# Reading order of the first matmul operand in a run: blocks from the end, in a chunked and in a Strassen-type product

## The chip, the cores and the metric

The kernel runs on one core of one Trainium2 chip. The metric is the device time of one execution in microseconds. The kernel before took 860.09 us (median of 3 runs, 858.67 to 861.0).

## The reference

```python
kv  = einsum('bhsd,bhse->bhde', k, v)             # (8, 8, 64, 64)
out = einsum('bhsd,bhde->bhse', q, kv)            # (8, 8, 576, 64)
rms = sqrt(mean(out * out, axis=-1) + 1e-6)
x   = (out / rms * g_norm)  ->  (4608, 512)       # heads side by side
h   = x @ w_in                                    # (4608, 2048)
g   = maximum(h, 0) + log1p(exp(-abs(h)))         # softplus
y   = g @ w_out                                   # (4608, 512)
```

Everything is 32 bits wide. The two large products need more precision than one pass gives, so every operand of them is kept as three parts (a high part, a rest and a combination of both), and every product is three matmuls that add up in PSUM.

## The kernel before

**Attention.** For each batch, `k` and `v` are multiplied into `kv` (line 696). For each tile of 128 tokens `q` is multiplied by `kv` (line 720), each head's row is normalised (VectorE, ScalarE, GpSimd), and the rows are turned so that features lie on the partitions (line 738 or VectorE). The turned x goes to DRAM and comes back split into three parts.

**The feed-forward block** has 2048 hidden columns in 16 chunks of 128, and is done in three passes over the tokens.

- The first phase (`step`) goes through 12 blocks of 384 tokens. Four blocks take 4 chunks each and eight take 6, so there are 64 steps, in the text "chunks". A chunk's first product `mm1` (line 864) is 12 matmuls of 128x384: 3 parts (`i`) times 4 slices of the 512 features (`kd`), numbered m = 0 to 11, all into one bank. ScalarE and VectorE make softplus and its three parts. The second product `mm2` (line 871) is 9 matmuls of 128x512, 3 for each of 3 tiles of tokens, and adds up over the chunks in banks of its own. In the steady part TensorE runs `mm1` of one chunk, `mm2` of an earlier one, `mm1` of the next, and so on.
- The two Strassen phases (`wide_step`) take the other chunks, two at a time, on 512 tokens. The first product is done with seven products of half size in place of eight (`product`, line 1066): each is 6 matmuls of 128x256, three parts (`m`) times two slices (`kd`). Between them ScalarE and VectorE copy and add banks. The second product (`mm2` inside `wide_step`, line 1137) is 3 matmuls of 128x512 for each of 2 chunks and 4 tiles of tokens. Products and second products are interleaved: a run of one, two or more products (6, 12 and more matmuls of 256 columns) stands between runs of second products. The text calls such a run of products a visit.

**The order of the work** is written by a planner (`Plan.order`): each task has an engine, an estimated duration, a position and the buffers it takes and gives, and the planner simulates the engines and issues the tasks in the order of its simulated starts. The instructions of each engine are then issued in that order. Within a task such as `mm1`, `product` or `mm2` the matmuls follow each other as the loops say.

**Reading orders.** Both the moving operand and the bank that is written can be run through in blocks from the end. The helper is

```python
def from_the_end(x, w):
    return x.rearrange("p (b w) -> p b w", w=w)[:, ::-1] if w else x
```

With `w` = 0 the columns are taken forward. With `w` = 16 they are taken in blocks of 16 words, last block first, each block forward. The same order is used for the operand and for the bank, so each result lands in the column where it belongs. Before the change, `mm1` reads m = 0 to 10 forward and m = 11 with `w` = 1 (word by word backward); the first-phase `mm2` reads forward; a Strassen product alternates `w` = 16 and 8 with `kd`; the Strassen `mm2` uses `w` = 128. Each matmul has its own weight load, which runs beside the matmul before it.

Further lines that the prediction names: 952 (`prime`, one 512-column matmul with the identity that clears a bank), 776, 525 and 526 (small matmuls of the attention part and of the weight preparation).

Of the kernel before, what the change touches and what calls it, by code (L numbers as in the profile page):

```python
# [18 lines left out]
P = 128  # L19
# [22 lines left out]
def from_the_end(x, w):  # L42

    return x.rearrange("p (b w) -> p b w", w=w)[:, ::-1] if w else x
# [16 lines left out]
class Plan:  # L61
# [19 lines left out]
    def slot(self, ring):  # L81
        return Slot(ring)

    def add(self, engine, ns, run, after=(), pos=0.0, take=(), give=(), size=0, behind=None, follows=None, kind="all"):
        pos, behind = round(pos, 4), None if behind is None else round(behind, 4)
        t = Task(engine, ns, run, [a for a in after if a is not None], pos, list(take), list(give), size)
        for s in t.give:
            s.readers += 1
        self.tasks.append(t)
        t.follows = follows  # L90
        t.behind = behind
        t.kind = kind
        return t
# [113 lines left out]
def kernel(  # L207
# [24 lines left out]
    nc = tc.nc  # L232
# [5 lines left out]
    KD, KF = d_model // P, d_ff // P  # L238
# [610 lines left out]
    def step(s):  # L849
        n, c = ORDER[s]  # L850
        cs = CHUNKS[n]
        h, g, gv = slot("h"), slot("g"), slot("gv")
        if c == cs[0]:
            sums[:] = [slot(f"s{i}") for i in range(TB)]
        xv, w_in, w_out = xv_slots[n], w_slots[0, c], w_slots[1, c]
        mine = list(sums)
        kept = c >= 4

        def mm1():
            hp = new(h, [P, NT])  # L860
            for m in range(3 * KD):
                i, kd = divmod(m, KD)
                w = 1 if m == 3 * KD - 1 else 0
                nc.tensor.matmul(from_the_end(hp, w), lhsT=w_in.tile[:, i, kd * P:(kd + 1) * P], rhs=from_the_end(xv.tile[:, i, kd], w),  # L864
                                 start=(m == 0), stop=(m == 3 * KD - 1))

        def mm2(i):
            if c == cs[0]:
                new(mine[i], [P, d_model])
            for m in range(3):  # L870
                nc.tensor.matmul(mine[i].tile, lhsT=gv.tile[:, m, i * P:(i + 1) * P], rhs=w_out.tile[:, m],  # L871
                                 start=(c == cs[0] and m == 0), stop=(c == cs[-1] and m == 2))

        def low():
            nc.vector.tensor_tensor(out=gv.tile[:, 1], in0=g.tile, in1=gv.tile.bitcast(F32)[:, 0], op=ALU.subtract)

        def less():
            f32 = gv.tile.bitcast(F32)
            nc.vector.scalar_tensor_tensor(out=gv.tile[:, 2], in0=f32[:, 1], scalar=-RADIX, in1=f32[:, 0],
                                           op0=ALU.mult, op1=ALU.add)  # L880

        a = add("PE", 2100, mm1, x_split[n] + factors_done[0, c] + [m for _, m in mm1s[-1:]] +
                (factors_done[1, ORDER[s - 2][1]] if s > 1 else []), s, [h],
                ([xv] if c == cs[-1] else []) + ([w_in] if s == last_step[c] and c != 4 else []))
        mm1s.append((s, a))
        a = add("ACT", 490, lambda: nc.scalar.activation(new(g, [P, NT]), h.tile, func=AF.Softplus, scale=1.0 + E),  # L886
                [a], s, [g], [h])
        a = add("ACT", 530, lambda: nc.scalar.activation(new(gv, [P, 3, NT], F32R)[:, 0], g.tile, func=AF.Copy, scale=DOWN),
                [a], s, [gv])
        a = add("DVE", 570, low, [a], s, [], [g])  # L890
        a = add("DVE", 570, less, [a], s)
        for i in range(TB):
            a2 = add("PE", 700, lambda i=i: mm2(i), [a] + factors_done[1, c] + [mm2s.get(i)], s + 1.5,
                     [mine[i]] if c == cs[0] else [],
                     [gv] + ([w_out] if s == last_step[c] and not kept else []))
            mm2s[i] = a2
            if c == cs[-1]:
                leave(0, n * TB + i, mine[i], a2, s + 1.5)
# [60 lines left out]
    def units_of(ph, n):  # L959
# [3 lines left out]
        for j, us in enumerate(GROUPS):  # L963
# [74 lines left out]
            for v, u in enumerate(us):  # L1038
                unit_slots[ph, n, u] = dst, v
                unit_done[ph, n, u] = [c]  # L1040

    PRODUCTS = [(0, 0), (1, 0), (0, 1), (1, 1), (2, 1), (2, 0), (3, 0)]

    def wide_step(k):
# [9 lines left out]
        def place(q):  # L1054
            return ab.tile[:, q // 2, q % 2 * HW:(q % 2 + 1) * HW]
# [3 lines left out]
        def product(u, q):  # L1059
            f, i = PRODUCTS[u]  # L1060
            w = forms[p][f].tile
            dst, v = unit_slots[ph, n, u]
            for m in range(3):
                for kd in range(2):
                    at = i * 2 * P + kd * P
                    nc.tensor.matmul(from_the_end(place(q), (16, 8)[kd]), lhsT=w[:, m, at:at + P],  # L1066
                                     rhs=from_the_end(dst.tile[:, m, v, kd] if u < 6 else dst.tile[:, m, kd], (16, 8)[kd]),
                                     start=(u == 0 and not m and not kd), stop=(m == 2 and kd == 1), skip_group_check=True)

        def multiply(u, q, after, pos, take=(), follows=None):  # L1070
            f = PRODUCTS[u][0]
            give = [unit_slots[ph, n, u][0]] if last else []
            if final and u in (2, 3, 5, 6):
                give.append(forms[p][f])
            return add("PE", 710, lambda: product(u, q), unit_done[ph, n, u] + forms_done[p][f] + list(after), pos, take, give,
                       follows=follows)
# [3 lines left out]
        def gt(dtype=F32):  # L1080
            if dtype not in held:
                held[dtype] = sb.tile([P, 2, WIDE], dtype, tag=f"g{gv.place}", name=f"g{gv.place}_{dtype == F32}")
            return held[dtype]

        def gvt(m, dtype=F32):
            y = gv.tile[:, m]
            return y if dtype == F32R else y.bitcast(F32)
# [8 lines left out]
        def begin():  # L1096
            new(ab, None)
            product(0, X)
# [31 lines left out]
            nc.vector.scalar_tensor_tensor(out=gt(F32R), in0=gvt(1), scalar=-RADIX, in1=gvt(0), op0=ALU.mult, op1=ALU.add)  # L1130

        def mm2(c, i):
            fresh = first and not c and ph < LAST
            if fresh:
                new(mine[i], [P, d_model])
            for m in range(3):
                nc.tensor.matmul(from_the_end(mine[i].tile, P), lhsT=(gvt(m, F32R) if m < 2 else gt(F32R))[:, c, i * P:(i + 1) * P],  # L1137
                                 rhs=from_the_end(outs[c].tile[:, m], P),
                                 start=fresh and not m, stop=(last and c == 1 and m == 2), skip_group_check=True)
# [21 lines left out]
        for c in range(2):  # L1161
            for i in range(TW):
                slot_pos = b + PACE + MM2[TW * c + i]
                a2 = add("PE", 700, lambda c=c, i=i: mm2(c, i),
                         [split_done[c]] + factors_done[1, 2 * p + c] + ([seeds[i]] if i in seeds and not c else []) +
                         ([before[i]] if c or not first else []), slot_pos, [mine[i]] if first and not c and ph < LAST else [], [gv] + ([outs[c]] if final else []))
                before[i] = a2
                if last and c:
                    leave(ph, TW * n + i, mine[i], a2, slot_pos)
# [98 lines left out]
```

## Time and profile before

| what | value |
|---|---|
| median of 3 runs | 860.09 us |
| lowest, highest run | 858.67, 861.0 us |
| profiled execution, time | 858.61 us |
| profiled execution, span from first to last instruction | 856.8 us |
| granted TensorE clock, mean | 1.000 |
| matmuls at line 864 (384 columns) | 768 |
| matmuls at line 871 (512 columns) | 576 |
| matmuls at line 1066 (256 columns) | 2016 |
| matmuls at line 1137 (512 columns) | 1152 |

All durations come from the profiled execution. The page lists the busy time of each engine, the chain of work that ended last (followed back from the last instruction), and groups of instructions by line with their tiles, shapes and counts. A line of the timeline has the start in microseconds from the span's start, the time that the group of successive instructions took to its last end, the engine, the line, the tiles and the count. Matmuls overlap: one starts before the one before it has ended, so the distance between two starts is what a matmul costs in a dense stream. The trace has each start to the nanosecond, and distances of single matmuls are from there. A few matmul records can be missing from a trace.

### The profile page before, as it was taken

What the parts mean: (1) busy time and instruction counts of PE and PEld (TensorE: products, weight loads), DVE (VectorE), ACT (ScalarE), POOL (GpSimd) and SP (SyncE); (2) the same over time, 40 slices, a digit from 0 to 9 for tenths busy, and PEclk for the clock granted to TensorE, in tenths of its full rate; (3) what the DMA queues carried; (4) which work ended last, traced back from release to release, by engine and by line L of the source; (5) the groups of instructions that cost most, each with busy time, mean ns of one, the idle gap of its engine ahead of it and who ended that gap; (6) DMA issues with size and microseconds to landing.
All of it is one profiled execution on the core that took longest, in us unless ns stands there. A gap on an engine that the chain in (4) does not pass through costs nothing.

```text
span 856.8 us, 17075 instructions
## 1 busy us (share of the span) xinstructions
PE 843.8 (98%) x6464; PEld 754.7 (88%) x6464; DVE 704.1 (82%) x995; ACT 520.2 (61%) x980; POOL 76.1 (9%) x79
## 2 busy tenths in 40 slices
PE   7899999999999999999999999999999999999998
PEld 5678898999898999998999999998999899999996
DVE  7988898888788889798898788878788766788873
ACT  6866665446344567776667665655868555566654
POOL 0342224111113300000000000000000000000000
PEclk9999999999999999999999999999999999999999
DMA  9998997778784755436645456645354753777864
GB/s 275 301 228 218 264 270 244 178 243 221 215 186 118 194 159 183 143 112 202 211 156 167 160 160 203 197 158 182 124 195 138 234 167 103 241 242 239 250 189 130
DMA packets 239778, 167.07 MB, mean 195 GB/s; under 512 B 106320, under 2 KB 198736, under 8 KB 239696
## 3 DMA queue, kind: packets, MB, share of 16 engines
q1 hardware_dynamic: 239392, 165.86, 65.8%
q8 instruction: 50, 0.82, 0.4%
q14 instruction: 32, 0.26, 0.1%
q10 hardware_dynamic: 304, 0.13, 0.1%
HBM read 112.98 MB, written 52.95 MB: 194 GB/s over the span
## 4 chain that ended last, share of the span: by engine, by line
PE 94%; DVE 2%; ACT 1%; DMA 1%; issue 1%; POOL 1%; SPq 0%; DVEq 0%; ACTq 0%
PE banks L1137 31%; PE banks L1066 28%; PE banks L871 16%; PE banks L864 15%; PE banks L720 2%; PE banks L696 2%; DMA loads<-in_v_dram 1%; DMA raw<-in_moe_w_in_dram 0%; PE banks L738 0%; POOL roots L728 0%; PE banks L1232 0%; DVE half L732 0%; DVE m L464 0%; DVE m L460 0%; DVE units L643 0%
## 5 line engine op out<-in xcount | busy, mean ns | idle before, releaser
L1137 PE MATMUL banks<-pieces,gv 128*128 128x512 f32 x768 | 236.8, 390 | 0.0
L1137 PE MATMUL banks<-pieces,g_False 128*128 128x512 f32 x384 | 149.4, 389 | 0.0
L1137 PEld LDWEIGHTS banks<-pieces,gv 128*128 128x128 f32 x768 | 132.5, 188 | 17.2 <-DVE banks L910 0.2
L864 PE MATMUL banks<-units,pieces 128*128 128x384 f32 x768 | 145.6, 338 | 0.0
L871 PE MATMUL banks<-pieces,gv 128*128 128x512 f32 x576 | 143.3, 393 | 0.0
L864 PEld LDWEIGHTS banks<-units,pieces 128*128 128x128 f32 x768 | 135.5, 188 | 4.5
L871 PEld LDWEIGHTS banks<-pieces,gv 128*128 128x128 f32 x576 | 106.2, 188 | 19.0
L1066 PEld LDWEIGHTS banks<-units,pieces 128*128 128x128 f32 x840 | 111.0, 188 | 6.5 <-ACT banks L1112 0.4
L1066 PE MATMUL banks<-units,pieces 128*128 128x256 f32 x840 | 115.2, 280 | 0.0
L886 ACT ACTIVATE half<-banks 128x384 f32<-128x384 f32 x64 | 31.4, 491 | 95.7 <-PE banks L864 89.8
L1127 DVE TENSOR_TENSOR gv<-g_True,gv 128x1024 fp32r<-128x1024 f32 x47 | 57.5, 1223 | 36.3 <-ACT gv L1124 36.3
L1137 PEld LDWEIGHTS banks<-pieces,g_False 128*128 128x128 f32 x384 | 72.1, 188 | 15.0
L1066 PEld LDWEIGHTS banks<-units,w 128*128 128x128 f32 x504 | 66.7, 188 | 3.7 <-ACT banks L1112 0.2
L1066 PE MATMUL banks<-units,w 128*128 128x256 f32 x504 | 69.6, 280 | 0.0
L728 POOL TENSOR_TENSOR roots<-roots,half 128x8 f32<-128x8 f32 x36 | 61.9, 1720 | 3.0
L1130 DVE SCALAR_TENSOR_TENSOR g_False<-gv 128x1024 fp32r<-128x1024 f32 x47 | 57.6, 1225 | 1.5
L1029 DVE TENSOR_TENSOR units<-loads,units 128x1024 fp32r<-128x1024 f32 x42 | 51.2, 1219 | 6.0 <-ACT units L1026 5.9
L1094 ACT ACTIVATE g_True<-banks 128x256 f32<-128x256 f32 x96 | 36.7, 384 | 30.6 <-PE banks L1066 29.9
L1116 DVE TENSOR_TENSOR g_True<-banks,g_True 128x512 f32<-128x512 f32 x48 | 33.1, 690 | 25.8 <-PE banks L1066 19.8
L931 ACT ACTIVATE m<-banks 128x512 f32<-128x512 f32 x72 | 42.1, 595 | 17.7 <-PE banks L1137 12.5
L1032 DVE SCALAR_TENSOR_TENSOR units<-units 128x1024 fp32r<-128x1024 f32 x42 | 51.4, 1224 | 1.7
L1026 ACT ACTIVATE units<-loads 128x1024 fp32r<-128x1024 f32 x42 | 44.4, 1056 | 12.7 <-PE banks L1066 10.1
(115 smaller groups left out, 1248.5 us busy)
## 6 DMA issues: line engine op xcount, KB each, us to landing
loads<-x SPq DMA_DIRECT2D x180, 128.0 KB, 2.7
part<-m SPq DMA_DIRECT2D x72, 256.0 KB, 2.9
m<-part SPq DMA_DIRECT2D x72, 256.0 KB, 3.5
loads<-form SPq DMA_DIRECT2D x45, 256.0 KB, 3.2
form<-loads SPq DMA_DIRECT2D x36, 256.0 KB, 3.0
raw<-in_moe_w_in_dram SPq DMA_DIRECT2D x16, 512.0 KB, 4.6
loads<-in_k_dram SPq DMA_DIRECT2D x32, 256.0 KB, 4.5
loads<-in_v_dram SPq DMA_DIRECT2D x32, 256.0 KB, 4.6
```

The lines of the kernel that those rows point to most:

```text
L728: nc.gpsimd.tensor_tensor(out=r.tile, in0=r.tile, in1=half, op=ALU.pow)
L864: nc.tensor.matmul(from_the_end(hp, w), lhsT=w_in.tile[:, i, kd * P:(kd + 1) * P], rhs=from_the_end(xv.tile[:, i, kd], w), start=(m == 0), ...
L871: nc.tensor.matmul(mine[i].tile, lhsT=gv.tile[:, m, i * P:(i + 1) * P], rhs=w_out.tile[:, m], start=(c == cs[0] and m == 0), stop=(c == cs ...
L931: a = add("ACT", 690 if ph == LAST else 600, lambda: nc.scalar.activation(new(ot, [P, d_model]), bank.tile, func=AF.Copy, scale=scale if p ...
L1026: nc.scalar.activation(part_of(0, F32R), xl.tile if m > 1 else xl.tile[:, 0], func=AF.Copy, scale=DOWN)
L1029: nc.vector.tensor_tensor(out=part_of(1, F32R), in0=xl.tile if m > 1 else xl.tile[:, 0], in1=part_of(0), op=ALU.subtract)
L1032: nc.vector.scalar_tensor_tensor(out=part_of(2, F32R), in0=part_of(1), scalar=-RADIX, in1=part_of(0), op0=ALU.mult, op1=ALU.add)
L1066: nc.tensor.matmul(from_the_end(place(q), (16, 8)[kd]), lhsT=w[:, m, at:at + P], rhs=from_the_end(dst.tile[:, m, v, kd] if u < 6 else dst. ...
L1094: nc.scalar.activation(dst, src, func=AF.Softplus, scale=1.0 + E)
L1127: nc.vector.tensor_tensor(out=gvt(1, F32R), in0=gt(), in1=gvt(0), op=ALU.subtract)
L1130: nc.vector.scalar_tensor_tensor(out=gt(F32R), in0=gvt(1), scalar=-RADIX, in1=gvt(0), op0=ALU.mult, op1=ALU.add)
L1137: nc.tensor.matmul(from_the_end(mine[i].tile, P), lhsT=(gvt(m, F32R) if m < 2 else gt(F32R))[:, c, i * P:(i + 1) * P], rhs=from_the_end(ou ...
```

## The change

The first matmul of each `mm1` (m = 0) is read and written in blocks of 4 words from the end; before, it was read forward. In the Strassen phases, the first 256-column matmul after any second product (and the very first one of all) is read and written in blocks of 64 words from the end; before, it had blocks of 16. A flag `long_before` is set at each `mm2` of `wide_step` and cleared by the next matmul of a product. All other matmuls keep their order. The number of instructions, their shapes, waits, buffers and the planner's order stay as they are.

```diff
             for m in range(3 * KD):
                 i, kd = divmod(m, KD)
-                w = 1 if m == 3 * KD - 1 else 0
+                w = 0 if 0 < m < 3 * KD - 1 else 1 if m else 4
                 nc.tensor.matmul(from_the_end(hp, w), lhsT=w_in.tile[:, i, kd * P:(kd + 1) * P], rhs=from_the_end(xv.tile[:, i, kd], w),
                                  start=(m == 0), stop=(m == 3 * KD - 1))
...
+    long_before = [True]
...
             for m in range(3):
                 for kd in range(2):
                     at = i * 2 * P + kd * P
-                    nc.tensor.matmul(from_the_end(place(q), (16, 8)[kd]), lhsT=w[:, m, at:at + P],
-                                     rhs=from_the_end(dst.tile[:, m, v, kd] if u < 6 else dst.tile[:, m, kd], (16, 8)[kd]),
+                    t = 64 if long_before.pop() else (16, 8)[kd]
+                    long_before.append(False)
+                    nc.tensor.matmul(from_the_end(place(q), t), lhsT=w[:, m, at:at + P],
+                                     rhs=from_the_end(dst.tile[:, m, v, kd] if u < 6 else dst.tile[:, m, kd], t),
                                      start=(u == 0 and not m and not kd), stop=(m == 2 and kd == 1), skip_group_check=True)
...
         def mm2(c, i):
+            long_before[:] = [True]
             fresh = first and not c and ph < LAST
```

## The prediction

> **What bounds the kernel.** I read the page's busy rows first, then the chain that ended last, then the groups by line, and then the timeline of TensorE in single stretches. The busy row and the chain agree:
>
> ```profile
> PE 843.8 (98%) x6464; PEld 754.7 (88%) x6464; DVE 704.1 (82%) x995; ACT 520.2 (61%) x980; POOL 76.1 (9%) x79
> ...
> PE 94%; DVE 2%; ACT 1%; DMA 1%; issue 1%; POOL 1%; SPq 0%; DVEq 0%; ACTq 0%
> PE banks L1137 31%; PE banks L1066 28%; PE banks L871 16%; PE banks L864 15%; PE banks L720 2%; PE banks L696 2%; DMA loads<-in_v_dram 1%; DMA raw<-in_moe_w_in_dram 0%; PE banks L738 0%; POOL roots L728 0%; PE banks L1232 0%; DVE half L732 0%; DVE m L464 0%; DVE m L460 0%; DVE units L643 0%
> ```
>
> TensorE is the path for 94% of the span, and four lines of matmuls hold 90% of it. The granted clock is 1.000 throughout. So the time is a sum of distances from the start of one matmul to the start of the next, and whatever the change does to such a distance goes into the total undiminished. The "mean ns of one" in the groups (338, 280, 390) does not help here: matmuls overlap, and it is longer than the distance. I therefore read distances from the start column of the timeline:
>
> ```profile
> 336.65 0.88 PE L1066 MATMUL banks<-early,pieces 128*128 128x256 f32 x6
> 337.37 2.23 PE L871 MATMUL banks<-pieces,gv 128*128 128x512 f32 x9
> 339.44 2.27 PE L864 MATMUL banks<-units,pieces 128*128 128x384 f32 x12
> 341.54 0.88 PE L1066 MATMUL banks<-early,pieces 128*128 128x256 f32 x6
> 342.26 2.25 PE L864 MATMUL banks<-units,pieces 128*128 128x384 f32 x12
> 344.34 4.24 PE L871 MATMUL banks<-pieces,gv 128*128 128x512 f32 x18
> ```
>
> Two chunks of the first phase stand here, and they differ: the 12 matmuls from 339.44 take 2.10 us, the 12 from 342.26 take 2.08. The next stretch is from the Strassen phases, around one short stop:
>
> ```profile
> 397.20 0.86 PE L1066 MATMUL banks<-early,w 128*128 128x256 f32 x6
> 397.90 0.97 PE L1066 MATMUL banks<-turned,half 128*128 128x256 f32 x6
> 398.71 1.60 PE L1066 MATMUL banks<-units,pieces 128*128 128x256 f32 x12
> 400.15 0.63 PE L1137 MATMUL banks<-pieces,gv 128*128 128x512 f32 x2
> ...
> 402.90 0.86 PE L1066 MATMUL banks<-early,pieces 128*128 128x256 f32 x6
> 403.60 0.39 PE L1137 MATMUL banks<-pieces,gv 128*128 128x512 f32 x1
> ```
>
> The first six products take 0.70 us, 117 ns each. After a stop of 0.1 us the twelve from 398.71 take 1.44 us, 120 each. After the next 512-column products it is 0.70 for six again. So products with the same reading order have two steady paces, and which one holds is decided where a run of them begins.
>
> **Distances, from the trace's single starts.** Steady: 173.3 ns for 384 columns, 226.7 for 512, 116.7 (or 120) for 256. At the full clock I see a surplus that doesn't grow with the width between 384 and 512 (53.3 ns for 128 more columns, so 160 and 213.3 of streaming, 13.3 over each), while 256 columns (106.7 by the same slope) stand at 10 over, or 13.3 in the slower pace.
>
> **Part 1, the first 384-column product (line 864, 64 chunks).** Nothing is added: the same 128x384 is read and the same bank is written, in another order; no wait, transfer or instruction is new. What can change is pace.
> - The order itself: products read forward (m = 6 to 10) and the one read word by word backward (m = 11) are both followed after 173 ns. Blocks of 4 words lie between these two orders: price 0.
> - What follows it: in 51 of the 64 chunks the distances run 171, 175, 178, 185, 176, 182 and then 173 for good: 26 ns more than at the steady pace. In the other 13, which follow small matmuls, a stop, the prime of line 952 or a visit of 256 columns, they run about 174, 175, 174, 173: 3 to 6 ns more (in some, a wait of 0.1 us before the second). That is the 2.10 against 2.08 above. A different start of the run ends the uneven stretch, and the change gives each run a different start. If all 51 lose it: 51 x 26 ns = 1.3 us. Bounds: best, the steady pace falls too (first rival); worst, the uneven stretch doubles, +1.3 us. I take -1.3, by the row of the 13 chunks.
>
> **Part 2, the first 256-column product of a visit (line 1066).** A visit here is a run of products after second products; the flag is set at each mm2. 164 such places stand in the trace right behind line 1137, and one at the very first visit: 165.
> - The order itself: the first product, in blocks of 16, is followed after 115.9 ns; blocks of 8 after 116.7; blocks of 128 words (line 1137, 512 columns) cost the same 226.7 as forward reading at line 871. 64 lies between 16 and 128: price 0. Bounds: at best 109 ns, the least distance between two weight loads around the stop at 397.9 (165 x 7 = -1.1 us); at worst 120 (165 x 4 = +0.7 us).
> - What follows it: behind 164 visits' starts the pace is already the better one nearly always. Over the 2016 products all surplus above 116.7 adds up to 0.5 us, most of it single waits. There is next to nothing to win at this pace, and the whole difference of the two paces to lose. I take 0.
>
> **One rule of the pages against the rows.** Blocks read from the end are not contiguous. The row is m = 11: read and written word by word backward, it is followed after 173 ns like its neighbours. The Trainium skill ("PSUM — Partial Sum Buffer", Specifications (TRN2)) says that any non-contiguous access pattern slows matmuls significantly, with lines of 8 bytes. The trace doesn't bear that out for reversed orders.
>
> **Sum.** The profiled execution took 858.61 us (span 856.8, 1.8 around it). 858.61 - 1.3 + 0 = 857.3. The median of the three runs shown, 860.09, is 1.5 above the profiled one; against it the forecast is **858.8**. That is 0.15% less, and about 0.3% (2.6 us) is what a measurement of this kernel can tell from no change. No wait takes the place of the lost 26 ns: TensorE's listed waits on others in the whole span come to about 9 us, none of them after 160 us, and a chunk that ends 26 ns sooner is followed by three 512-column matmuls whose inputs were ready (line 871's idle time is 0.0).
>
> **Rivals.**
> 1. **A better steady pace in the first phase.** For: 256 columns show that a surplus of 10 ns instead of 13.3 exists, and that the start of a run picks the pace. If the 384-column runs settle at 170: 768 x 3.33 = 2.6 us, with the 1.3 above 3.9: 860.09 - 3.9 = 856.2. Against: the 51 and the 13 chunks begin differently and all end at 173.3. A Strassen pace lower by another 3.33 ns would give 2016 x 3.33 = 6.7 us (853.4 alone); no row shows one.
> 2. **The Strassen visits fall into the slower pace: slower than before.** The changed product is the very one behind which a run settles. If the order in blocks of 64 shifts its start as the stop at 397.9 did, every visit runs at 120 until its next 512-column products: 2016 x 3.33 = 6.7 us, less the some 50 products that are there already (0.2): 860.09 + 6.5 = 866.6, or 865.3 with part 1's gain. It decides visit by visit: with part 1's gain, the total is slower by 0.3% from about 60% of the visits on. For: every run in the trace that begins otherwise than after steady 512-column products (after a stop, at 336.65 and 341.54 behind 384-column ones with 0.72 us for six, behind the prime at 354.85) begins at 120. Against: a delay of 13 ns inside a visit at 652.1 leaves the pace at 117, and the four orders seen cost alike.
> 3. **The change does nothing that counts.** The uneven stretch is set by what runs before the chunk and not by m = 0. 860.1. Against: what differs between 51 and 13 chunks is only how the run begins.
> 4. **Non-contiguous reading is slow after all.** If each changed product took twice its distance: 64 x 173 + 165 x 117 = 30 us, 890. That is what the rule of the PSUM page would come to at such a price; the row of m = 11 is against it.
>
> **Chances.** The forecast (uneven stretch gone, Strassen unmoved) 0.30; rival 3 0.10; rival 1 0.28, of which 0.06 for a better Strassen pace; rival 2 0.31; rival 4 0.01. The forecast and rival 3 are within 0.3%: 0.40; faster by over 0.3%: 0.28; slower: 0.32. The forecast's own range is 857.5 to 860.3. The range that should hold it 8 times in 10 reaches to rival 1 in the first phase and to rival 2: 855.6 to 866.8.
>
> **What would show it.** Each is a distance between start times in the changed kernel's timeline. Part 1 right: the 12 products of nearly every chunk take 2.08 us instead of 2.10; rival 1: 2.04; rival 3: 2.10 in 51 chunks as now. Part 2 right: six products 0.70 us after each 512-column run; rival 2: 0.72, six after six, until the next 512-column products. Line 1137 stays at 227 ns and line 871 as well; if those distances move, the steps above are wrong, because I count only on the runs that begin with a changed product. A first product of 230 or 340 ns would be rival 4. New waits of TensorE on ScalarE or VectorE would mean that the slack behind TensorE was thinner than I read it.

## The result, and the profile after

The changed kernel takes 866.36 us (median of 6 runs, 865.27 to 868.32) against 859.8 (6 runs, 858.67 to 861.0): a ratio of 1.0081, 95% interval 1.0069 to 1.0093. It is slower by 0.8%. The profiled execution took 865.87 us, with a span of 864.1 (before 856.8) at a clock of 1.000.

The page of the changed kernel still shows TensorE as the path. Lines 1066 and 1137 have become 1069 and 1141:

```profile
PE 849.4 (98%) x6464; PEld 757.7 (88%) x6464; DVE 704.4 (82%) x995; ACT 521.7 (60%) x980; POOL 76.4 (9%) x79
...
PE 95%; DMA 3%; DVE 1%; ACT 1%; SPq 0%; POOL 0%; issue 0%; POOLq 0%; DVEq 0%; ACTq 0%
PE banks L1141 31%; PE banks L1069 28%; PE banks L871 15%; PE banks L864 15%; PE banks L696 2%; PE banks L720 2%; DMA loads<-in_k_dram 1%; DMA loads<-in_v_dram 1%; PE banks L1236 0%; PE banks L738 0%; DMA w<-in_q_dram 0%; PE banks L776 0%; DVE half L732 0%; SPq L685 0%; POOL roots L728 0%
```

The shares of the four lines hardly differ. DMA has 3% of the chain in place of 1%: TensorE's listed waits come to 10.3 us in place of 8.8, and what was added lies before 44 us, where k, v and q are loaded. The first chunk begins only 0.3 us later (44.07 against 43.75), and after 160 us no wait is listed in either kernel. The rest of the added time lies in the matmuls themselves. Where it lies comes out when the distances from each start to the next are added up by line, and the steady pace of the width (173.3 ns for 384 columns, 226.7 for 512, 116.7 for 256) is taken off:

| line (before) | columns | matmuls | over the steady pace, before | after | change |
|---|---|---|---|---|---|
| 864, first product of a chunk | 384 | 768 | 3.61 us | 2.87 us | -0.74 us |
| 871, second product of a chunk | 512 | 576 | 3.84 | 3.85 | 0.0 |
| 1066, Strassen products | 256 | 2016 | 0.49 | 4.71 | +4.22 |
| 1137, Strassen second products | 512 | 1152 | 0.46 | 3.90 | +3.44 |

The sum is +6.9 of the 7.3 us between the spans; all other lines together give +0.3. The timeline after, at the chunks shown of before (start, time to the last end, engine, line, tiles, count):

```profile
336.96 2.23 PE L871 MATMUL banks<-pieces,gv 128*128 128x512 f32 x9
339.02 2.25 PE L864 MATMUL banks<-units,pieces 128*128 128x384 f32 x12
341.11 0.88 PE L1069 MATMUL banks<-early,pieces 128*128 128x256 f32 x6
341.82 2.27 PE L864 MATMUL banks<-units,pieces 128*128 128x384 f32 x12
343.94 0.39 PE L871 MATMUL banks<-pieces,gv 128*128 128x512 f32 x1
```

The chunk behind 512-column products now takes 2.09 us (before 2.10), but the one behind a Strassen product takes 2.12 (before 2.08). At the visit around 397 us:

```profile
397.24 0.87 PE L1069 MATMUL banks<-early,w 128*128 128x256 f32 x6
397.94 0.95 PE L1069 MATMUL banks<-turned,half 128*128 128x256 f32 x6
398.73 1.60 PE L1069 MATMUL banks<-units,pieces 128*128 128x256 f32 x12
400.17 0.63 PE L1141 MATMUL banks<-pieces,gv 128*128 128x512 f32 x2
...
402.93 0.87 PE L1069 MATMUL banks<-early,pieces 128*128 128x256 f32 x6
403.64 0.63 PE L1141 MATMUL banks<-pieces,gv 128*128 128x512 f32 x2
```

Six products are too short to show much (0.71 against 0.70). A visit of 24 products shows the loss whole. Before:

```profile
414.62 0.86 PE L1066 MATMUL banks<-units,w 128*128 128x256 f32 x6
415.31 2.26 PE L1066 MATMUL banks<-units,pieces 128*128 128x256 f32 x18
417.42 0.62 PE L1137 MATMUL banks<-pieces,gv 128*128 128x512 f32 x2
...
419.45 0.86 PE L1066 MATMUL banks<-units,w 128*128 128x256 f32 x6
```

After:

```profile
414.87 0.87 PE L1069 MATMUL banks<-units,w 128*128 128x256 f32 x6
415.57 2.32 PE L1069 MATMUL banks<-units,pieces 128*128 128x256 f32 x18
417.73 0.63 PE L1141 MATMUL banks<-pieces,gv 128*128 128x512 f32 x2
...
419.80 0.87 PE L1069 MATMUL banks<-units,w 128*128 128x256 f32 x6
```

The 24 products took 2.80 us and now take 2.86, and the nine 512-column products behind them 2.07 in place of 2.04. The distances from start to start in this visit are now 112, 116, 119, 119, 121, 117 ns and then 121 and 119 in turn. The only product whose order was changed is the first, and it has become the cheapest; the products after it, whose order is as before, pay. In the 512-column products behind, the distances run 231, 235, 229, 232, 231 and then 227.

### The profile page after: what moved, and what is told of

Same layout as the page of the kernel before. It is cut to its first block, busy times and chain, and to the rows that moved or that the text cites. A ratio compares the mean times of both kernels' runs of the same rounds, so it can differ in the third digit from the quotient of the medians.

```text
span 864.1 us, 17075 instructions
## 1 busy us (share of the span) xinstructions
PE 849.4 (98%) x6464; PEld 757.7 (88%) x6464; DVE 704.4 (82%) x995; ACT 521.7 (60%) x980; POOL 76.4 (9%) x79
## 4 chain that ended last, share of the span: by engine, by line
PE 95%; DMA 3%; DVE 1%; ACT 1%; SPq 0%; POOL 0%; issue 0%; POOLq 0%; DVEq 0%; ACTq 0%
PE banks L1141 31%; PE banks L1069 28%; PE banks L871 15%; PE banks L864 15%; PE banks L696 2%; PE banks L720 2%; DMA loads<-in_k_dram 1%; DMA loads<-in_v_dram 1%; PE banks L1236 0%; PE banks L738 0%; DMA w<-in_q_dram 0%; PE banks L776 0%; DVE half L732 0%; SPq L685 0%; POOL roots L728 0%
## 5 line engine op out<-in xcount | busy, mean ns | idle before, releaser
L1069 PE MATMUL banks<-units,pieces 128*128 128x256 f32 x840 | 116.8, 282 | 0.0
```

The lines of the kernel that those rows point to most:

```text
L1069: nc.tensor.matmul(from_the_end(place(q), t), lhsT=w[:, m, at:at + P], rhs=from_the_end(dst.tile[:, m, v, kd] if u < 6 else dst.tile[:, m, ...
```

## The experiments

Theory K at the start: the reading order of a run's first product moves the point from which the run settles. The rivals were that the order itself is slow (O), that the fast pace belongs to the pair 16 and 8 alone (A), and that the two parts of the change act together. Kernels that ran only once ("one run") are judged by the distances in their traces; the runs of the kernel before beside them lie between 858.25 and 862.38 us. Lines are named by their numbers in the kernel before, except in the lines of the timelines. "Over" means over the steady pace, added up as in the table above. From the second experiment on the first phase is as before the change, but for the last one.

**The first-phase part alone.**

```diff
-                w = 1 if m == 3 * KD - 1 else 0
+                w = 0 if 0 < m < 3 * KD - 1 else 1 if m else 4
```

> Only the first-phase part of the change: m = 0 of each first product in blocks of 4 words, Strassen visits as before. Theory K (the order of the first product moves the start of a run, and the run settles from there; the two parts are independent): the first phase loses 0.7 to 0.9 us as in the changed kernel, Strassen lines stay at 116.7 and 226.7 ns, time 0.1% below before. Rival (the loss is spread by the whole change, or the changed first phase disturbs what follows): above before.

858.61 us (11 runs) against 859.75 (15): ratio 0.9993, interval 0.9984 to 1.0002. Line 864 stands at 2.87 us over the steady pace, lines 1066 and 1137 at 0.48 and 0.46. The time cannot tell it from before, the trace can: -0.74 us at line 864 and nothing elsewhere.

**The Strassen part alone.**

```diff
-                    t = (16, 8)[kd]
+                    t = 64 if long_before.pop() else (16, 8)[kd]
```

> Only the Strassen part: the first 256-column product of a visit in blocks of 64. Theory K: all of the loss is here, 7 to 8 us above before, of it some 4.2 us at line 1066 and some 3.4 us at the 512-column products behind the visits. Rival: part of the loss stays away, because it needs the changed first phase as well: under 5 us above before.

867.01 us (4 runs) against 859.75 (15): ratio 1.0085, interval 1.0071 to 1.0099. Line 1066 is 4.71 and line 1137 3.89 over. The whole loss is here; the parts are independent.

**The first product forward.** `t = 0 if long_before.pop() else (16, 8)[kd]`

> First 256-column product of a visit read forward instead of in blocks of 16; all else as before. Theory K (any order of the first product that differs from its successors moves the start): visits slower as in the changed kernel, 2 to 8 us above before. Rival O (the order in blocks of 64 is itself slow): forward costs nothing, time as before within 0.3%.

One run: 866.17 us; lines 1066 and 1137 are 4.68 and 3.90 over, the distances those of blocks of 64. Forward and blocks of 64 act alike, so O falls: it had forward cost nothing.

**Every product of kd = 0 in 64.** `t = (64, 8)[kd]`

> Every Strassen product alternates 64 and 8 instead of 16 and 8, so that the first one is no exception. Theory K: with no odd one out a run settles as before, time as before within 0.3%. Rival O (64 is slow in itself): 1008 matmuls have it instead of 165, so the loss grows, over 10 us above before. Rival A (the fast pace needs the pair 16 and 8): every visit at 120 ns throughout, 6 to 7 us above before at line 1066.

One run: 860.59 us, span 857.0. Line 1066 is 0.04 us below the steady pace and line 1137 0.77 over: first product 113 ns, then 116.7, and the first 512-column product 230 in place of 227. A falls as well: 16 is not needed. A first 64 is harmless where 64 and 8 follow. From this came theory M: a run keeps the fast pace where its first product has the order of those that follow. Its rival F: a first 16 is good and a first 64 is bad, whatever follows.

**All products forward.** `t = 0`

> Every Strassen product read forward, first phase as before. Theory M (a run keeps the fast pace where the first product of a slice has the order of the products after it, whatever that order): 116.7 ns throughout, line 1137 at 227, time within 0.3% of before. Rival A (the fast pace comes from the alternation of a larger and a smaller block): the visits run near 120 and the 512-column products behind them pay too, 6 to 10 us above before.

One run: 869.43 us; line 1066 is 5.34 and line 1137 3.97 over. After some uneven distances at the start of a visit (113 and 119 in most visits of six, 117, 118, 119, 121, 117 and 117 in many longer ones) the products stand at 120. Theory M, as it was put there (any order will do if the first agrees with the rest), is wrong: equal orders throughout are slow. Orders that differ between kd = 0 and 1 are needed, and 16 and 8 are not the only pair. Rival A in the wider form that it has here (a larger block and a smaller one in turn) came out as expected; that such a pair is not enough is shown by the 25 pairs below, where (32, 8) settles at 120.

**The mirror: first 16, then 64 and 8.** `t = 16 if long_before.pop() else (64, 8)[kd]`

> The mirror of the change: products alternate 64 and 8, only the first of a visit has 16. Theory M: mismatched again, so the loss returns, 5 to 9 us above before. Rival F (a first product in 16 is good and one in 64 or forward is bad, whatever follows): as before within 0.3%.

One run: 859.28 us; line 1066 is 0.14 us below the steady pace and line 1137 0.80 over. A mismatch in this direction costs nothing, so M falls for good; F is right about a first 16, but the kernel with 64 throughout kept its pace with a first 64. What loses the pace is a first 64 (or forward) with (16, 8) behind it, and not a first product that is different. With that Theory K is wrong as well where it says that any different first product moves the start.

**Read and write apart.** In two kernels only one side of the first product has blocks of 64; columns of it then land in other places.

```diff
-nc.tensor.matmul(from_the_end(place(q), t), ..., rhs=from_the_end(..., t), ...)
+nc.tensor.matmul(from_the_end(place(q), (16, 8)[kd]), ..., rhs=from_the_end(..., t), ...)      # first kernel
+nc.tensor.matmul(from_the_end(place(q), t), ..., rhs=from_the_end(..., (16, 8)[kd]), ...)      # second kernel
```

> As the Strassen part of the change, but the first product of a visit has blocks of 64 for the operand that is read only; the bank is written in blocks of 16 as before, so columns of that product land in other places and the output is not the reference's. If the read from SBUF makes the effect: 7 us above before with the distances of the changed kernel. If the write into PSUM makes it: as before. If both must agree: something else.

> The opposite: the first product of a visit writes the bank in blocks of 64 and reads its operand in blocks of 16, so columns land in other places and the output is not the reference's. If the write into PSUM makes the effect: 7 us above before. If the read from SBUF makes it: as before.

Operand alone: 866.76 us, lines 1066 and 1137 are 4.73 and 3.91 over. Bank alone: 0.59 and 0.52 over, as before; its 861.98 us (span 860.2) comes from a mean clock of 0.92 in the first 45 us, before any matmul that the edit touches (its first chunk begins at 46.87 us, 3.1 later than before). The visit of 24 products, operand alone:

```profile
415.75 0.87 PE L1069 MATMUL banks<-units,w 128*128 128x256 f32 x6
416.46 2.32 PE L1069 MATMUL banks<-units,pieces 128*128 128x256 f32 x18
418.62 0.63 PE L1141 MATMUL banks<-pieces,gv 128*128 128x512 f32 x2
```

Bank alone:

```profile
417.82 0.86 PE L1069 MATMUL banks<-units,w 128*128 128x256 f32 x6
418.52 2.26 PE L1069 MATMUL banks<-units,pieces 128*128 128x256 f32 x18
420.62 0.62 PE L1141 MATMUL banks<-pieces,gv 128*128 128x512 f32 x2
```

24 products take 2.87 us with the operand in 64 and 2.80 with the bank in 64. The whole effect is in the order in which the operand is read from SBUF. Theory R took over, so far only argued: the phase between TensorE's own two read streams, operand and weights, sets the pace.

**Trains behind the kernel.** To the kernel before, runs of matmuls are appended: 18 of 512 columns, 18 of 256 in a chosen order, and so on.

```python
def train(first, pair, cols=P, n=18):
    for i in range(n):
        m, kd = i // 2 % 3, i % 2
        t = first if not i else pair[kd]
        nc.tensor.matmul(from_the_end(banks[:cols, 0, :HW], t), lhsT=wt[:, m, kd * P:kd * P + cols],
                         rhs=from_the_end(mv[:, m, 0, kd], t), start=not i, stop=True, skip_group_check=True)
```

> The kernel before with trains of matmuls appended behind its work, when the other engines stand still: 18 products of 512 columns, then 18 of 256 in a chosen reading order, and so on (19 trains; three of them with weight loads of 64 columns, half as wide), then 9 of 512 forward and 12 of 384 with different first orders (7 trains). Their results are not used, and the total time means nothing; distances of starts are read. Theory R (the phase between TensorE's own two read streams, operand and weights, sets the pace): the trains repeat the kernel's paces without any other engine: first 16 then 16 and 8 at 116.7 ns, first 64 or forward then 16 and 8 near 119 to 120 with a dear start of the 512-column products after it, all forward 120; first 16 then 64 and 8 at 116.7; with half as wide weight loads the orders no longer differ. 384 columns: first forward has the uneven stretch of 26 ns, first in 4 has 3 to 6. Rival (reads or writes of other engines make the difference): all trains at one pace, whatever the order.

From 858.2 us on every engine but TensorE is idle. The first trains are 16 then (16, 8); 64 then (16, 8); and (16, 16):

```profile
858.20 2.26 PE L1254 MATMUL banks<-units,pieces 128*128 128x256 f32 x18
860.30 4.24 PE L1246 MATMUL banks<-pieces 128*128 128x512 f32 x18
864.38 2.31 PE L1254 MATMUL banks<-units,pieces 128*128 128x256 f32 x18
866.52 4.27 PE L1246 MATMUL banks<-pieces 128*128 128x512 f32 x18
870.63 2.28 PE L1254 MATMUL banks<-units,pieces 128*128 128x256 f32 x18
```

18 products last 2.10 us (116.7 each) in the first train and 2.14 in the second; the 18 products of 512 behind them 4.08 and 4.11. So the kernel's two paces come without work of another engine, and the rival with other engines falls. By the distances between starts:

| first, then (kd 0, kd 1) | mean of 18 | the 512-column products behind |
|---|---|---|
| 16 or 32, then (16, 8) | 116.6 ns | 227 from the start |
| 64, 128, then (16, 8): identical | 119.3 | 231, 236, 228, 232, 231, then 227 |
| 8, then (16, 8) or (8, 8): identical | 119.7 | 230, 236, 229, 232, 231, then 227 |
| 4, then (16, 8) | 119.6 | nine uneven ones, 224 to 236 |
| 0 or 16, then (64, 8) | 116.5 | 230, then 227 |
| 16, then (8, 16) | 116.8 | ten uneven ones, 224 to 236 |
| (16, 16) | 117.8 | seven uneven ones, 224 to 236 |
| (32, 16) | 118.3 | ten uneven ones, 225 to 236 |
| (0, 0) and (64, 64): identical | 119.6 | 233, 236, 229, 232, 231, then 227 |
| (4, 4) and (1, 1): identical | 118.2 | 235, 231, then 227 |

The trains with half as wide weight loads (64 columns) answer differently from what was expected. All forward runs at 113.3 ns in the end. By the slope between 384 and 512 columns (53.3 ns for 128 more) the streaming of 256 columns takes an estimated 106.7, so the surplus is 6.7 instead of 13.3. But 16 and 8 stay at 116.7, so the orders still differ, the other way round. A load of 64 columns lasts 135 ns in the trace and one of 128 lasts 188. These trains also write half as many partitions of the bank, so they do not show that it is the weight load that makes the surplus, and Theory R stays an argument; why a pair is good or bad is not shown either.

The trains of 384 columns: first forward 171, 175, 178, 185, 176, 181, then 173 (mean of 12: 175.5); first in blocks of 4 or of 1 word 174, 176, 174, 175, then 173 (173.8); 16 in between (174.4); 64 as forward. With a forward last product (m = 11) the nine 512-column products behind it average 231.2 instead of 226.7 or 226.8 ns; that is what its backward order is worth in the trains.

**All pairs.** Trains in the same manner for all 25 pairs out of forward, 32, 16, 8 and 4, at 256, 384 and 512 columns.

> The kernel before with trains appended behind its work, as in the kernel with 26 trains: all 25 pairs of reading orders out of forward, 32, 16, 8 and 4 words, taken in turn, for 18 products of 256 columns, 12 of 384 and 12 of 512, each behind 12 products of 512 in blocks of 128. Their results are not used, and the total time means nothing. Theory R (the operand's reads and the weight loads meet in a pattern that depends on both orders): the pairs fall on a few paces and not on one; 16 then 8 and 64-like then 8 are at 116.7 for 256 columns, equal orders near 120; orders of 384 and 512 columns, whose weight load covers only part of the product, move by at most the same surplus of 13 ns. A pair below 116.7, 173.3 or 226.7 would be a better version. Rival (16 then 8 is the only good pair, and wider products do not care): all other pairs at 120, all of 384 and 512 at 173.3 and 226.7.

No pair beats the steady paces. At 256 columns (forward, 8), (forward, 32) and (16, 8) cost nothing in all, with the 512-column products behind them counted; the other pairs cost 33 to 100 ns in a train of 18. At 384 columns the pairs settle at 173.3 to 180, forward at 173.3. Forward is not the cheapest there in all: with its uneven stretch and the products behind it a train of 12 costs 67 ns, one of (forward, 8) costs 20. At 512 columns forward is best at 226.7, and pairs go up to 236.7. The move is at most 10 ns, and (8, forward) has the good pace but leaves 53 ns to the products behind it. Rival A's "only good pair" and "wider products do not care" both fall.

**First in 32.** `t = 32 if long_before.pop() else (16, 8)[kd]`

> The first 256-column product of a visit in blocks of 32 instead of 16; all else as before. Theory R, with the paces of the appended trains: a first 32 before 16 and 8 kept 116.7 ns there, so here too, time as before within 0.3%, line 1137 at 226.7. Rival (any odd one out costs the run its pace): 866 to 867 us as with 64, 128 or forward.

One run: 858.06 us; lines 1066 and 1137 are 0.41 and 0.47 over, as before. The trains foretold this. Which first orders are harmless was found by trying: 16 and 32 before (16, 8), forward, 64 and 16 before (64, 8). No run shows a rule behind it.

**Blocks of 4 only behind 512-column products.** Each task of TensorE writes into a flag whether it was a second product of the first phase, and `mm1` takes its first order from that.

```diff
+            start = behind[0]
...
-                w = 1 if m == 3 * KD - 1 else 0
+                w = 1 if m == 3 * KD - 1 else 0 if m else start
```

> Of the change only the first-phase part, and only where the task before on TensorE is a 512-column second product; the other chunks begin forward as before. Theory R: some 43 chunks lose their uneven stretch (26 to about 4 ns) and none gains one: about 1.0 us below before at line 864, a ratio near 0.999. Rival (what is saved is given back behind it): line 871 grows, time as before.

858.2 us (11 runs) against 860.17 (15): ratio 0.9983, interval 0.9974 to 0.9992, the one version that is measurably faster than before. Line 864 is 2.77 us over (before 3.61), line 871 unmoved at 3.89. The trace accounts for 0.8 us of it; the rest of the measured 0.17% (1.5 us) is within the interval.

## Why the prediction was wrong

- **Bound, unit of account and place: right.** TensorE carries the time, no wait was added after 160 us, and the difference is one of distances between starts.
- **Part 1, "I take -1.3": right kind, too large.** 0.74 us were saved. Of the 51 uneven chunks 46 became even, but at 5 to 11 ns over the steady pace (waits at their ends left aside) and not 3 to 6, and the prediction overlooked that the new start would spoil chunks that began well: six of the 13 (those behind small matmuls, the prime or a Strassen product) now have the uneven stretch. It reasoned that "a different start of the run ends the uneven stretch" and applied it to one group alone.
- **Part 2, "64 lies between 16 and 128: price 0 ... What follows it: ... I take 0": this is the step that failed.** Measured: +4.22 us at line 1066. The first product by itself went down, from 115.7 to 114.2 ns on average where no wait follows it, so the bounds for the order itself held. What failed is the value for the products behind it, which was set at nothing because the pace there was already good. That was a reason why nothing could be gained, not a reason why nothing would be lost; the prediction itself wrote "the whole difference of the two paces to lose" beside it, and gave rival 2 a chance of 0.31, no less than the forecast's 0.30. And the interpolation between 16 and 128 mixed two places: blocks of 128 had been seen only in 512-column runs. In front of (16, 8) a first product in 128 is as bad as one in 64 (in the trains) or forward (in the kernel), and one in 32 as good as one in 16.
- **Rival 2 is what happened, with another sum.** Its mechanism (a run falls to the slower pace until the next 512-column products) is there, but a visit's first products are still fast: a visit of six products pays 7.5 ns on average and one of 24 pays 62, not 20 and 80. So line 1066 lost 4.2 us and not 6.5. The prediction also stated that line 1137 stays at 227, because it counted only runs that begin with a changed product. That was wrong: the 512-column products take up to nine distances to settle again, most often five, and 73 of the 165 runs of them are only three products long. This term, which neither the forecast nor rival 2 had, measured 3.44 us. The errors partly cancel: the rival's 865.3 with part 1's gain comes near the 866.36 by luck, and so does the upper end of the range, 866.8, which was set by rival 2.
- **The kernel before showed the second term.** Behind each of the few visits that already ran at the slower pace, its 512-column products begin unevenly: behind the stop at 397.9 with 230, 236, 229, 232 and 231 ns. The prediction read the pace of such visits and not what stands behind them. At another such place before the change, six products take 0.71 us, and the first two 512-column products behind them take 0.46 (231 and 236 ns) where two steady distances make 0.45:

```profile
366.89 0.88 PE L1066 MATMUL banks<-units,w 128*128 128x256 f32 x6
367.60 0.63 PE L1137 MATMUL banks<-pieces,gv 128*128 128x512 f32 x2
368.06 0.39 PE L1137 MATMUL banks<-pieces,g_False 128*128 128x512 f32 x1
368.29 0.63 PE L1137 MATMUL banks<-pieces,gv 128*128 128x512 f32 x2
```

- **Rival 1** did not occur; no pair of orders in the trains is below the steady paces. **Rival 3** is refuted in both phases. **Rival 4** is refuted: no order doubles a product; among the 25 pairs the dearest single distance is 240 ns at 512 columns, where 226.7 is steady.

## What to carry to other kernels

In a dense stream of matmuls a product's cost is the distance to the next start, and it depends on what ran before: an edit to one product in a run has to be priced over all products up to the next settled stretch, in both directions. When a trace shows two steady paces and the kernel is on the better one, an edit at the place where the pace is chosen has little to win and the whole difference to lose; that should have turned the forecast. A train of the disputed shapes appended behind the kernel, with every other engine idle, answers such questions for dozens of variants in one run.

## What the runs showed of the hardware

- TensorE's steady distance in this kernel was 116.7 or 120 ns for 256 columns, 173.3 for 384 and 226.7 for 512 (other pairs of orders settle at up to 120, 180 and 236.7 in the trains). Which one holds at 256 depends on the order in which SBUF is read, not on the order in which PSUM is written (4.73 against 0.59 us over the steady pace).
- Orders fall into classes: trains with 64 and 128, or with 64 and forward, in the same place agreed to the nanosecond of rounding, and so did trains with 4 and 1. As far as these trains go, blocks of 64 words and more are no change of order for the pace.
- Read forward at 256 columns, the estimated surplus over streaming is 13.3 ns with 128 columns of weights and 6.7 with 64 (distances of 120 and 113.3). The Trainium skill ("TensorE: Matmul & The Clock Gate", Step-by-step: what each phase is for) says that loading the next tile's weights does not steal SBUF read bandwidth from the running matmul. The smaller surplus speaks against that if the weight load makes the surplus; no run here shows that it does, since the same trains wrote half as many partitions.
- The state outlives the run that made it: behind a slow visit it takes up to nine products of 512 columns, most often five, to return to 226.7.
- Open: what pattern of reads makes (16, 8), (64, 8) and (forward, 32) free and equal orders dear. No run varied the place of weights and operands in SBUF.
